# Banks dealt anew after attention, weight totals on GpSimd, small copies begun by GpSimd

## The chip, the cores and the metric

The kernel runs on one core of a Trainium2 chip. The metric is the device time of one execution in microseconds. Engines: TensorE (PE; its weight loads are PEld), VectorE (DVE), ScalarE (ACT), GpSimd (POOL), and SyncE (SP), which only begins transfers here. Each runs its instructions in the order in which they stand in its queue.

## The reference

Three stages follow one another, on 4 batches of 576 tokens with 512 features:

```python
scores = where(block_i >= block_j, q @ k.T / 8, -1e9)      # 8 heads of 64, blocks of 64
x  = softmax(scores) @ v                                   # heads side by side: (4, 576, 512)
x  = x + relu(layernorm(x) * g_ln @ w1a) @ w2a             # first FFN, 512 -> 2048 -> 512
u  = x + real(fft(fft(x, axis=1), axis=2))                 # Fourier mixing
out = u + relu(layernorm(u) @ w1b) @ w2b                   # second FFN
```

q, k, v are float32; the four weight matrices are float64, and nothing is converted on the host.

## The kernel before, in words

**Tiles.** The 2304 tokens are nine chunks of 256: for each batch b, E(b) holds tokens 0 to 255 and F(b) tokens 320 to 575 in mirrored order; L holds the 64 tokens between them of all four batches. An operand of TensorE is split into a high and a low float16 part, and a product is three passes (high-high, high-low, low-high).

**FFN.** For each chunk GEMM 1 (`gemm1`, line 482) runs in eight units mp of 24 matmuls. ScalarE writes the high half of the hidden tile hT (L491), VectorE the low half (L492). GEMM 2 (`gemm2`, L507; `gemm2_both`, L537, both 128-token halves at once, for E0 and F3 of the first FFN and E0 of the second) runs 48 matmuls a half, and VectorE adds the result to the tokens (L522). The first FFN's order is E0 E1 E2 E3 F0 F1 L F2 F3.

**Weights.** Each matrix comes in four chunks c of four pieces of 512 KB. A piece is loaded by SP (L161), decoded to float32 by two ScalarE passes (L173, L186) and two VectorE passes (L190, L193) and squared by ScalarE (L203), which gives partial sums "wn". When a chunk is whole, `w_scale` forms its total "wt" and a power-of-two scale "wsc" (`pow2`, L585 to L597); `w_hi` (L270) and `w_lo` (L279) write the two halves "wq". The total is taken by GpSimd's all-reduce (`all_sum`, L135) for the second FFN, and for the first FFN by a matmul with a tile of ones (L224), whose result lies in a PSUM buffer of tag "o". Staged chunks "ws" and scaled chunks "wq" share nine buffers of tag "w". The first FFN's eight chunks fill eight of them. Of the second FFN, two chunks of the first matrix go to DRAM and back once scaled, and those of the second matrix go there unscaled.

**Attention.** First the E chunks (`e_items`: scores L683, exponentials L701, probabilities P turned by a DMA transpose to PT, then pv, L631), while the first FFN's weights are decoded. Then, in a new SBUF pool, the other tokens (`attention_items`, scores L843, pv L631), beside which the first FFN runs chunk by chunk. `e_v` scales a batch's v by an all-reduced total "et".

**Fourier stage.** For each batch, `dft_a1` folds E and F, takes a total "dt" by all_sum, and splits the folded tokens to "ge", "gL" and "g0s"; five small SBUF copies (L1060, L1090) collect rows of gL and g0s in the tile gS. `dft_a2` multiplies ge and gS by cosine and sine matrices (ya, L1110), ScalarE and VectorE evacuate y (L1114, L1115), and `dft_b_main` does the second axis (pq, pf; L1131, L1141).

**PSUM.** Eight banks: pool psg, tag "g", two buffers of one bank (GEMM 1 and GEMM 2); pss, tag "s", two buffers of two banks (scores; later ya, pq, pf); pso, tag "o", two of one bank (pv, wt of the first FFN). all_sum's results are tiles of tag "ar" in the pool sm, which has two buffers.

**What sets the order.** The kernel's streams (E attention, weights, FFN, main attention, Fourier stage, second weights) are lists of items (planned time, function, needs, gives); `merge` calls the item with the smallest planned time next. The order of these calls is the order of the program text, and so of the priorities. The tile framework's planner then sets each engine's queue by a model of times; a buffer of a tag is given to the tiles in the order of the text. E attention of batch 0 starts at planned time 0, of batch 1 at 25, of 2 and 3 at 50; the first FFN's weights at 20, 1.6 a piece; the second matrix follows the first. The second FFN's weights start at 300, 4 a piece, and need the last attention result X1 L.

Of the kernel before, what the change touches and what calls it, by code (L numbers as in the profile page):

```python
# [8 lines left out]
F32 = mybir.dt.float32  # L9
F16 = mybir.dt.float16  # L10
# [7 lines left out]
DM = H * D  # L18
# [40 lines left out]
GB = 2  # L59
WT = ((2, 1), (2, 2))  # L60
S_E1 = 25.0
# [22 lines left out]
def fused_kernel(ctx: ExitStack, tc: tile.TileContext, io: dict):  # L84
# [8 lines left out]
    dram = ctx.enter_context(tc.tile_pool(name="dram", bufs=1, space=bass.MemoryType.DRAM))  # L93
    pss = ctx.enter_context(tc.tile_pool(name="pss", bufs=2, space=PS))
    pso = ctx.enter_context(tc.tile_pool(name="pso", bufs=4 - GB, space=PS))

    gcol = cpool.tile([128, KT], F32, name="gcol")
    gmax = cpool.tile([128, 1], F32, name="gmax")

    ones = cpool.tile([128, 128], BF16, name="ones")  # L100
    late = cpool.tile([128, 3, 128], BF16, name="late")
# [76 lines left out]
    def w_decode(ffn, which, c, i, n):  # L178
# [28 lines left out]
        )  # L207

    def w_scale(ffn, which, c):

        n2 = W.pop(("n2", ffn, which, c))
        n = n2.shape[-1]
        if (ffn, which) in WT:
            if n > 1:
                n1 = sm.tile([128, 1], F32, tag="wn1", bufs=2, name="wn1")
                nc.vector.tensor_reduce(out=n1, in_=n2, axis=AX.X, op=ALU.add)
                n2 = n1
            tot = all_sum(n2, 1, "wt")
        else:
            nb = sm.tile([128, n], BF16, tag="wnb", bufs=2, name="wnb")  # L220
            nc.vector.tensor_copy(out=nb, in_=n2)
            tot = pso.tile([128, 1], F32, tag="o", name="wt")
            for i in range(n):
                nc.tensor.matmul(  # L224
                    out=tot, lhsT=ones, rhs=nb[:, i:i + 1], start=(i == 0), stop=(i == n - 1)
                )
# [23 lines left out]
    def w_jobs(ffn, which, c):  # L250
# [5 lines left out]
        return [(st[:, i:i + m, :].rearrange("p i f -> p (i f)"), i, i + m, s) for i in range(0, 4, m)]  # L256

    def w_hi(ffn, which, c):
        if ffn == 2 and which == 1:
            t = wst["pool"].tile([128, 2, 2048], F16, tag="w", bufs=2, name=f"wq{ffn}{which}{c}")  # L260
        else:
            t = wpool.tile([128, 2, 2048], F16, tag="w", bufs=9, name=f"wq{ffn}{which}{c}")
# [10 lines left out]
        W["t", ffn, which, c] = t  # L273

# [16 lines left out]
    def w_second():  # L291


        out = []

        def piece(which, c, i):
            n = WN[1]
            w_load(2, which, c, i, n)
            w_raw(2, which, c, i, n)
            w_decode(2, which, c, i, n)  # L300
            if i + n < 4:
                return
            w_scale(2, which, c)
            if which == 1:
                w_hi(2, 1, c)
                w_lo(2, 1, c)
                if c >= 2:
                    t = W.pop((2, 1, c))
                    w_spill(t.rearrange("p a f -> p (a f)"), (2, 1, c), F16)
            else:  # L310
                st = W.pop(("st", 2, 2, c))
                w_spill(st.rearrange("p i f -> p (i f)"), (2, 2, c), F32)

        for which, order in ((1, (2, 3, 0, 1)), (2, (0, 1, 2, 3))):
            for c in order:
                for i in range(0, 4, WN[1]):
                    last = i + WN[1] == 4
                    gives = ("W", 2, 1, c) if which == 1 and last and c < 2 else None
                    if (which, c) == (2, 3) and last:
                        gives = ("W2", "dram")  # L320
# [4 lines left out]
        return out  # L325

# [16 lines left out]
    def w_items():  # L343

        n = WN[0]
        pieces = [(which, c, i) for which in (1, 2) for c in range(4) for i in range(0, 4, n)]

        def load(k):
            if k < len(pieces):
                w_load(1, *pieces[k], n)  # L350

        def piece(k):
# [4 lines left out]
            if i + n == 4:  # L357
                w_scale(1, which, c)
                if which == 1:
                    w_hi(1, which, c)  # L360
                    w_lo(1, which, c)

        def end(c):
            if c == 0:
                w_balance(1)
            w_hi(1, 2, c)
            w_lo(1, 2, c)

        first = [(0.0, lambda k=k: load(k), (), None) for k in range(PL)]
        out = ([], [])  # L370
        for k, (which, c, i) in enumerate(pieces):
            gives = ("W", 1, 1, c) if which == 1 and i + n == 4 else None
            out[which - 1].append((float(n), lambda k=k: piece(k), (), gives))
        for c in range(4):
            out[1].append((1.0, lambda c=c: end(c), (), ("W", 1, 2, c)))
        return first, out[0], out[1]
# [83 lines left out]

    def gemm1(ffn, c, mp, side=False):
        if mp == 0:
# [8 lines left out]
        xt = xnT[ffn, c]  # L471
        if side:
            ps = pss.tile([128, 2, 512], F32, tag="s", name="g1s")[:, 0, :]
            ps = ps.rearrange("p (i n) -> p i n", i=2)
        else:
            ps = psg.tile([128, 2, 256], F32, tag="g", name="g1")
        for i in range(2):
# [21 lines left out]
    def gemm2(ffn, c, t, part, nparts=4):  # L499
        if part == 0:  # L500
            g2[0] = psg.tile([128, DM], F32, tag="g", name="g2")
        ps = g2[0]
# [26 lines left out]
    def gemm2_both(ffn, c, part):  # L529

        if part == 0:
            g2["b"] = [psg.tile([128, DM], F32, tag="g", name="g2") for _ in range(2)]
        h = hT[ffn, c]
# [40 lines left out]
    def a_close():  # L574
        ap_["ctx"].close()
# [476 lines left out]
    def dft_left_split(b, s):  # L1052
# [43 lines left out]
    def dft_a2(b, blk):  # L1096
# [73 lines left out]
    def dft_b_main(b, t):  # L1170
# [3 lines left out]
        ks = slice(128 * t, 128 * t + 128)  # L1174
        pq = pss.tile([128, 512], F32, tag="s", name="pq")
        dft_b(lambda f, a: y[:, f, a, ks], lambda a: y5[:, 289 * a + 128 * t:289 * a + 128 * t + 128],
              lambda f, a: y[0:128 - f, 2 + f, a, ks], pq)
        pf = None
        if t == 0:

            pf = pss.tile([128, 512], F32, tag="s", name="pf")
            w = lambda f, a: slice(289 * (2 * f + a) + 288, 289 * (2 * f + a) + 416)
            dft_b(lambda f, a: yw[:, w(f, a)], lambda a: y5[:, w(0, a)], None, pf)
        dft_apply(pq, pf, inv[:, 0:1], X["E", b][:, t, :], X["F", b][:, t, :])

    def dft_b_left():
        yl, yl5 = D_["yl"], D_["yl5"]
        pq = pss.tile([128, 512], F32, tag="s", name="pql")
        dft_b(lambda f, a: yl[:, f, a, :], lambda a: yl5[:, a, :],
# [12 lines left out]
    if True:  # L1202
# [4 lines left out]
        nc.gpsimd.partition_all_reduce(gmax, g2c[:, KT:], 128, bass_isa.ReduceOp.max)  # L1207
        nc.vector.memset(ones, 1.0)
        nc.vector.memset(late, 0.0)
# [19 lines left out]
        def a_end():  # L1229
            a_close()  # L1230
            dft_setup(dctx)

# [10 lines left out]
        def ffn_items(ffn, order, both=(), mixed=None):  # L1243
            seq = []
            for n, c in enumerate(order):
# [3 lines left out]
                if ffn == 1 and n < LNA:  # L1249
# [6 lines left out]
                g1 = [  # L1256
                    (2.62, lambda mp=mp, c=c: gemm1(ffn, c, mp, c == mixed), (("W", ffn, 1, mp // 2),) + g1_needs,
                     ("G1", ffn, c, mp)) for mp in range(8)
# [170 lines left out]
```

## Time and profile before

| | us |
|---|---|
| median of 3 runs | 1056.16 (1055.52 to 1056.41) |
| profiled execution, its own time | 1056.17 |
| its span, first to last instruction | 1054.3 |
| TensorE busy | 943.6 (89%) |
| VectorE busy | 624.7 (59%) |
| ScalarE busy | 506.5 (48%) |
| GpSimd busy | 70.1 (7%) |

The page divides the span into 40 slices; the digit of an engine is the tenth of a slice in which it was busy, and 9 is 90% or more. A timeline row gives start, duration, engine, line, operation, tiles (out<-in), count, and in brackets the idle time before it with what ended that. A releaser is the last event by the profile; where it had long been done, the true one was another.

### The profile page before, as it was taken

To read this page: it belongs to the slowest core of one execution; us is meant where nothing else is said; L and a number is where in the kernel's file an instruction comes from. 1 tells how busy PE (TensorE), PEld (TensorE's weight loads), DVE (VectorE), ACT (ScalarE), POOL (GpSimd) and SP (SyncE) were. 2 spreads that over 40 slices of the span, in tenths; PEclk is the share of its full clock that TensorE was granted. 3 is DMA by queue.
4 is the path that set the end of the run, shared out by engine and by line. 5 is a ranking of instruction groups with operands and counts; after the bars stand their busy time and mean duration, and the time that the engine had idled before them with its cause. 6 is when DMAs were issued, how large, how long until landed. Compare 5 with 4: busy or idle time off the path is not lost.

```text
span 1054.3 us, 18458 instructions
## 1 busy us (share of the span) xinstructions
PE 943.6 (89%) x7234; PEld 644.3 (61%) x7234; DVE 624.7 (59%) x1542; ACT 506.5 (48%) x916; POOL 70.1 (7%) x190
## 2 busy tenths in 40 slices
PE   5375859998989898996999879999999999999998
PEld 4354744476566574764665655848577576585674
DVE  5778888777778876765368969864332322222210
ACT  6677876767677677525356665622111021111110
POOL 2000001001102002040000010000000000000000
PEclk9686988999999999998999999999999999999999
DMA  7887745566858657465205266520100110101100
GB/s 197 191 212 200 213 118 127 123 111 132 147 123 158 127 135 153 84 121 181 63 10 162 97 200 232 195 80 1 41 21 21 31 30 21 30 21 31 30 11 21
DMA packets 172647, 110.84 MB, mean 105 GB/s; under 512 B 146909, under 2 KB 155494, under 8 KB 171024
## 3 DMA queue, kind: packets, MB, share of 16 engines
q1 hardware_dynamic: 170880, 105.81, 40.7%
q0 software_dynamic: 1680, 3.85, 1.7%
q8 instruction: 57, 0.93, 0.4%
q14 instruction: 30, 0.25, 0.1%
HBM read 59.95 MB, written 11.01 MB: 67 GB/s over the span
## 4 chain that ended last, share of the span: by engine, by line
PE 42%; DVE 8%; DMA 5%; ACT 4%; issue 1%; POOL 0%; SPq 0%; ACTq 0%; POOLq 0%; DVEq 0%
PE g L507 19%; PE g L482 18%; DMA wr<-in_w 5%; PE g L537 2%; DVE wq L279 1%; ACT wr L203 1%; DVE ws L193 1%; ACT sign L186 1%; DVE hT L492 1%; ACT ws L173 1%; DVE ws L190 1%; PE st L843 1%; PE pv L631 1%; PE ya L1110 1%; ACT wq L270 0%
## 5 line engine op out<-in xcount | busy, mean ns | idle before, releaser
L482 PEld LDWEIGHTS <-wq 128*128 128x128 f16 x3456 | 339.6, 99 | 77.6 <-issue 27.0
L507 PE MATMUL g<-wq,hT 128*128 128x512 f16 x1440 | 331.3, 379 | 1.4 <-DVE hT L492 1.4
L507 PEld LDWEIGHTS <-hT 128*128 128x128 f16 x1440 | 139.7, 98 | 158.8 <-DVE hT L492 1.7
L491 ACT ACTIVATE hT<-g 128x512 f16<-128x512 f32 x144 | 84.7, 590 | 253.7 <-PE g L482 253.6
L492 DVE SCALAR_TENSOR_TENSOR hT<-g,hT 128x512 f16<-128x512 f32 x144 | 98.9, 688 | 145.8 <-ACT hT L491 145.8
L631 PE MATMUL pv<-vh,PT 128*128 128x65 f16 (+1 forms) x800 | 106.7, 204 | 26.3 <-DMA PT<-P 22.8
L631 PEld LDWEIGHTS <-PT 128*128 128x128 f16 x1200 | 84.3, 101 | 59.0 <-DMA PT<-P 32.5
L843 PE MATMUL st<-k,qz 128*128 128x512 f16 (+2 forms) x288 | 80.2, 338 | 11.6 <-ACT e L865 11.6
L656 DVE SCALAR_TENSOR_TENSOR P<-e,P 128x768 f16<-128x768 f32 (+2 forms) x64 | 62.0, 972 | 33.9 <-ACT P L655 33.5
L865 ACT ACTIVATE e<-st,aq,acf 128x384 f32<-128x384 f32 (+2 forms) x80 | 57.2, 742 | 50.1 <-DVE aq L860 46.3
L537 PE MATMUL g<-wq,hT 128*128 128x512 f16 x288 | 65.6, 387 | 5.2 <-ACT wq L270 3.3
L631 PE MATMUL pv<-vl,PT 128*128 128x64 f16 (+1 forms) x400 | 66.5, 203 | 0.0
L186 ACT ACTIVATE sign<-wr 128x512 f16<-128x512 f32 x64 | 49.1, 774 | 19.2 <-DMA wr<-in_w 14.0
L655 ACT ACTIVATE P<-e 128x768 f16<-128x768 f32 (+2 forms) x64 | 54.6, 858 | 3.4 <-DMA PT<-P 1.7
L173 ACT ACTIVATE ws<-wr 128x512 f32<-128x512 f32 x64 | 41.3, 667 | 31.0 <-DMA wr<-in_w 28.4
L683 PE MATMUL st<-raw 128*128 128x128 f32 (+1 forms) x128 | 39.2, 446 | 17.9 <-ACT e L701 7.5
L439 ACT ACTIVATE xs<-xn 128x512 f16<-128x512 f32 x36 | 22.5, 628 | 65.3 <-DVE xn L431 6.6
L445 DVE TENSOR_TENSOR xs<-xn,xs 128x512 f16<-128x512 f32 x36 | 24.7, 690 | 48.1 <-ACT xs L439 48.0
L537 PEld LDWEIGHTS <-hT 128*128 128x128 f16 x288 | 28.5, 99 | 39.0 <-issue 7.7
L190 DVE SCALAR_TENSOR_TENSOR ws<-ws,sign 128x512 int32<-128x512 int32 x64 | 43.3, 685 | 14.8 <-ACT sign L186 13.5
L859 DVE TENSOR_REDUCE aq<-st 128x2 f32<-128x768 f32 (+2 forms) x48 | 46.7, 973 | 0.8 <-PE st L843 0.8
L203 ACT ACTIVATE wr<-ws 128x512 bf16<-128x512 f32 (+1 forms) x40 | 35.2, 879 | 23.2 <-DVE ws L193 20.3
(387 smaller groups left out, 1291.2 us busy)
## 6 DMA issues: line engine op xcount, KB each, us to landing
wr<-in_w SPq DMA_DIRECT2D x64, 512.0 KB, 4.5
rawv<-in_vt SPq DMA_DIRECT2D x16, 320.0 KB, 3.8
rawqk<-in_kt SPq DMA_DIRECT2D x16, 288.0 KB, 2.8
out<-out SPq DMA_DIRECT2D x18, 256.0 KB, 2.0
d<-ws SPq DMA_DIRECT2D x4, 1024.0 KB, 5.5
ws<-d SPq DMA_DIRECT2D x4, 1024.0 KB, 6.8
rawqk<-in_qt SPq DMA_DIRECT2D x32, 80.0 KB, 3.7
raw<-in_qt SPq DMA_DIRECT2D x16, 128.0 KB, 3.8
```

What stands on the lines that cost most here:

```text
L186: nc.scalar.activation(out=z[:, :, :, 1], in_=hw.bitcast(F32), func=AF.Copy, scale=float(2.0 ** -100))
L190: nc.vector.scalar_tensor_tensor(out=di, in0=di, scalar=3, in1=zi, op0=ALU.logical_shift_left, op1=ALU.bitwise_or)
L482: nc.tensor.matmul(out=ps[:, i, :], lhsT=w1(ffn, k, wh, m), rhs=xt[:, xh, k, :], start=(n == 0), stop=(n == 3 * KT - 1),)
L491: nc.scalar.activation(out=h[:, :, 0, :], in_=ps, func=AF.Relu)
L492: nc.vector.scalar_tensor_tensor(out=h[:, :, 1, :], in0=ps, scalar=0.0, in1=h[:, :, 0, :], op0=ALU.max, op1=ALU.subtract,)
L507: nc.tensor.matmul(out=ps, lhsT=h[f // 4][:, f % 4, hh, t * 128:(t + 1) * 128], rhs=w2(ffn, f, wh), start=(f == 0 and hh == 0 and wh == 0) ...
L537: nc.tensor.matmul(out=g2["b"][t], lhsT=h[f // 4][:, f % 4, hh, t * 128:(t + 1) * 128], rhs=w2(ffn, f, wh), start=(f == 0 and hh == 0 and ...
L631: nc.tensor.matmul(out=out[..., 0:w], lhsT=l, rhs=v[..., 0:w], start=(n == 0), stop=(n == len(mm) - 1))
L655: nc.scalar.activation(out=P[:, 0, 0:n], in_=e, func=AF.Copy, scale=PSC)
L656: nc.vector.scalar_tensor_tensor(out=P[:, 1, 0:n], in0=e, scalar=PSC, in1=P[:, 0, 0:n], op0=ALU.mult, op1=ALU.subtract)
L843: nc.tensor.matmul(out=st[:, h, 0:n] if j < 4 else sf[:, o:o + n], lhsT=qz[:, a, q:q + 128], rhs=k[:, c, o:o + n], start=(i == 0), stop=(j ...
L865: nc.scalar.activation(out=e[:, h], in_=st[:, h], func=AF.Exp, scale=cf, bias=nb[:, h:h + 1],)
```

## The change

After attention (`ps_switch`, called from `a_end`) the pools pss and pso are closed; their six banks become psx (GX = 3 banks, for GEMM tiles) and psd (8 - 2 - 3 = 3 single banks, for the Fourier stage). GEMM tiles then go round 2 banks of psg and 3 of psx.

`w_scale` is cut in two. `w_total` takes the total by GpSimd for all weights, at the chunk's last piece. The scale and `w_hi`, `w_lo` follow one piece later, in `scales` (first FFN) and `end` (second FFN); the plan gives a chunk to its users one piece later. The tile of ones and the matmuls of L224 are gone.

The five copies to gS of a batch are begun by GpSimd, not SP. The argument `side` of gemm1 was not in use.

```diff
-WT = ((2, 1), (2, 2))
+GX = 3
-    pss = ctx.enter_context(tc.tile_pool(name="pss", bufs=2, space=PS))
-    pso = ctx.enter_context(tc.tile_pool(name="pso", bufs=4 - GB, space=PS))
+    pctx = ctx.enter_context(ExitStack())
+    pss = pctx.enter_context(tc.tile_pool(name="pss", bufs=2, space=PS))
+    pso = pctx.enter_context(tc.tile_pool(name="pso", bufs=4 - GB, space=PS))
+    psn = {"n": 0}
+    def g_tile(shape, name):
+        pool = psg
+        if "x" in psn:
+            pool = psn["x"] if psn["n"] % (GB + GX) >= GB else psg
+            psn["n"] += 1
+        return pool.tile(shape, F32, tag="g", name=name)
+    def d_tile(name):
+        return psn["d"].tile([128, 512], F32, tag="s", name=name)
+    def ps_switch():
+        pctx.close()
+        psn["d"] = pctx.enter_context(tc.tile_pool(name="psd", bufs=8 - GB - GX, space=PS))
+        psn["x"] = pctx.enter_context(tc.tile_pool(name="psx", bufs=GX, space=PS))
...
+    def w_total(ffn, which, c):
+        n2 = W.pop(("n2", ffn, which, c))
+        if n2.shape[-1] > 1:
+            n1 = sm.tile([128, 1], F32, tag="wn1", bufs=2, name="wn1")
+            nc.vector.tensor_reduce(out=n1, in_=n2, axis=AX.X, op=ALU.add)
+            n2 = n1
+        W["tot", ffn, which, c] = all_sum(n2, 1, "wt")
+        if which == 1:
+            W["t", ffn, which, c] = w_tile(ffn, which, c)
     def w_scale(ffn, which, c):
...
+        tot = W.pop(("tot", ffn, which, c))
...
         def piece(which, c, i):
             w_load(2, which, c, i, n)
             w_raw(2, which, c, i, n)
             w_decode(2, which, c, i, n)
+            end()
             if i + n < 4:
                 return
-            w_scale(2, which, c)
+            w_total(2, which, c)
...
+            todo.append((which, c))
+        def end():
+            for which, c in todo:
+                w_scale(2, which, c)
+                if which == 1:
+                    w_hi(2, 1, c)
+                    w_lo(2, 1, c)
...
         def piece(k):
             w_decode(1, which, c, i, n)
+            scales()
             if i + n == 4:
+                w_total(1, which, c)
+                todo.append((which, c))
...
-        ps = psg.tile([128, 2, 256], F32, tag="g", name="g1")
+        ps = g_tile([128, 2, 256], "g1")
...
-            nc.sync.dma_start(out=st[32 * i:32 * i + 32], in_=g[q, a])
+            nc.gpsimd.dma_start(out=st[32 * i:32 * i + 32], in_=g[q, a])
...
-            nc.sync.dma_start(out=st[96 + a:97 + a, 0:257], in_=g0s[:, a])
+            nc.gpsimd.dma_start(out=st[96 + a:97 + a, 0:257], in_=g0s[:, a])
...
-        ps = pss.tile([128, 512], F32, tag="s", name="ya")
+        ps = d_tile("ya")
...
         def a_end():
             a_close()
+            ps_switch()
             dft_setup(dctx)
```

## Rows read from the trace of the kernel before

**Rows 1.** The page's slices, TensorE's busy tenths (26.4 us a slice).
```profile
PE   5375859998989898996999879999999999999998
```
**Rows 2.** Windows: stretch, its length, each engine's busy time, granted clock, DMA.
```profile
0.00:159.00 159.00, 98.65 (x837) 80.06 (x838) 123.27 (x342) 119.17 (x211) 14.57 (x47) 0.83 0.75 188
184.00:460.00 276.00, 256.11 (x2414) 174.06 (x2412) 206.58 (x517) 189.69 (x342) 28.96 (x76) 0.99 0.65 127
481.00:515.20 34.20, 24.34 (x194) 20.14 (x192) 17.12 (x30) 19.43 (x37) 0.40 (x1) 0.85 0.42 137
515.20:552.00 36.80, 36.07 (x232) 22.33 (x231) 19.59 (x45) 15.87 (x28) 0.75 (x2) 1.00 0.08 18
552.00:688.00 136.00, 120.98 (x862) 85.30 (x862) 115.72 (x293) 87.58 (x173) 11.38 (x32) 0.99 0.53 176
```
**Rows 3.** Timeline of TensorE, GEMM 1 of L.
```profile
481.10 2.78 PE L482 MATMUL g<-xnT1L,wq 128*128 128x256 f16 x24
493.23 16.14 PE L482 MATMUL g<-xnT1L,wq 128*128 128x256 f16 x120 [9.35 <-DVE XxF L522]
...
515.22 20.88 PE L507 MATMUL g<-wq,hT 128*128 128x512 f16 x96
```
**Rows 4.** Timeline of VectorE in the same stretch.
```profile
478.18 0.75 DVE L522 SCALAR_TENSOR_TENSOR XxF<-g,winv,XxF 128x512 f32<-128x512 f32 x1
...
492.43 0.75 DVE L522 SCALAR_TENSOR_TENSOR XxF<-g,winv,XxF 128x512 f32<-128x512 f32 x1
...
496.78 0.69 DVE L492 SCALAR_TENSOR_TENSOR hT<-g,hT 128x512 f16<-128x512 f32 x1 [0.73 <-ACT hT L491]
...
506.77 0.16 DVE L216 TENSOR_REDUCE wn<-wn 128x1 f32<-128x4 f32 x1 [0.25 <-ACT wr L203]
```
**Rows 5.** Timeline of GpSimd, the all-reduces from 480 to 545 us.
```profile
487.83 0.40 POOL L135 PARTITION_ALL_REDUCE wt<-wn  x1 [17.38 <-DVE wn L216]
542.82 0.40 POOL L135 PARTITION_ALL_REDUCE dt<-dn  x1 [54.59 <-DVE dn L1072]
543.11 0.46 POOL L135 PARTITION_ALL_REDUCE wt<-wn  x1
```
**Rows 6.** Timeline of ScalarE, the first piece after chunk 3.
```profile
552.41 1.22 ACT L173 ACTIVATE ws<-wr 128x512 f32<-128x512 f32 x2 [1.39 <-DVE wq L279]
```
**Rows 7.** Timeline of TensorE, two starts between 552 and 688.
```profile
631.65 1.32 PE L1131 MATMUL pq<-c_cd,y 128*128 128x257 f16 x6 [3.81 <-DVE pw L594]
...
687.82 20.89 PE L537 MATMUL g<-wq,hT 128*128 128x512 f16 x96 [1.34 <-DVE hT L492]
```
**Rows 8.** Timeline of TensorE, totals of weight chunks five, seven and eight.
```profile
118.50 0.16 PE L224 MATMUL wt<-wnb,ones 128*128 128x1 bf16 x1
...
142.84 0.17 PE L224 MATMUL wt<-wnb,ones 128*128 128x1 bf16 x1
...
153.70 0.16 PE L224 MATMUL wt<-wnb,ones 128*128 128x1 bf16 x1 [3.44 <-DVE wnb L221]
154.51 0.23 PE L631 MATMUL pv<-vh,PT 128*128 128x65 f16 x1 [0.65 <-DMA PT<-P]
```
**Rows 9.** Timeline of SP, the main attention's first load.
```profile
168.58 0.33 SPq L767 DMA_DIRECT2D rawqk<-in_kt  x1
```
**Rows 10.** Timeline of GpSimd, et of batches 2 and 3.
```profile
65.07 0.39 POOL L135 PARTITION_ALL_REDUCE et<-en  x1 [1.28 <-ACT vh L640]
...
91.92 0.53 POOL L135 PARTITION_ALL_REDUCE et<-en  x1 [5.26 <-ACT vh L640]
```
**Rows 11.** SP's waits; groups by line; DMA issues with KB and us to landing.
```profile
SPq L1060 <- ACT g0s L1026: 33.4, 3, 25.4
...
L937 POOL DMA_DIRECT2D XxF<-N x24 | 14.0, 587 | 41.8 <-DVE N L910 31.4 <-DVE aq L860 8.2 <-ACT N L916 1.6
...
XxF<-N POOLq DMA_DIRECT2D x8, 126.0 KB, 3.8
gS<-gL SPq DMA_DIRECT2D x12, 32.0 KB, 2.0
```

More of the change, by code (lines that the diff above doesn't have):

```diff
@@ L207, in w_decode @@
         )
-    def w_scale(ffn, which, c):
[L211 to L226, printed above, removed]
+    def w_total(ffn, which, c):
[7 more added lines that the diff above has]
+            W["t", ffn, which, c] = w_tile(ffn, which, c)
+    def w_scale(ffn, which, c):
+        tot = W.pop(("tot", ffn, which, c))
         if (ffn, which) == (1, 1):
@@ L256, in w_jobs, with w_tile @@
         return [(st[:, i:i + m, :].rearrange("p i f -> p (i f)"), i, i + m, s) for i in range(0, 4, m)]
+    def w_tile(ffn, which, c):
+        if ffn == 2 and which == 1:
+            return wst["pool"].tile([128, 2, 2048], F16, tag="w", bufs=2, name=f"wq{ffn}{which}{c}")
+        return wpool.tile([128, 2, 2048], F16, tag="w", bufs=9, name=f"wq{ffn}{which}{c}")
     def w_hi(ffn, which, c):
[L259 to L262, printed above, removed]
+        if which == 2:
+            W["t", ffn, which, c] = w_tile(ffn, which, c)
+        t = W["t", ffn, which, c]
         if ffn == 1 and which == 1:
@@ L272, in w_hi @@
             )
-        W["t", ffn, which, c] = t
     def w_lo(ffn, which, c):
@@ L294, in w_second @@
         out = []
+        todo = []
         def piece(which, c, i):
@@ L300, in piece @@
             w_decode(2, which, c, i, n)
+            end()
             if i + n < 4:
                 return
-            w_scale(2, which, c)
[L304 to L310, printed above, removed]
+            w_total(2, which, c)
+            if which == 2:
                 st = W.pop(("st", 2, 2, c))
                 w_spill(st.rearrange("p i f -> p (i f)"), (2, 2, c), F32)
+            todo.append((which, c))
[5 more added lines that the diff above has]
+                    w_lo(2, 1, c)
+                    if c >= 2:
+                        t = W.pop((2, 1, c))
+                        w_spill(t.rearrange("p a f -> p (a f)"), (2, 1, c), F16)
+            todo.clear()
         for which, order in ((1, (2, 3, 0, 1)), (2, (0, 1, 2, 3))):
@@ L316, in w_second @@
                 for i in range(0, 4, WN[1]):
[L317 to L320, printed above, removed]
+                    gives = None
+                    if i == 0 and (which, c) in ((1, 1), (2, 0)):
+                        gives = ("W", 2, 1, 0 if which == 1 else 1)
                     needs = (("X1", "L"),)
@@ L324, in w_second @@
                     ))
-        return out
+        return out + [(0.0, end, (), ("W2", "dram"))]
     def w_back(c):
@@ L350, in load @@
                 w_load(1, *pieces[k], n)
+        todo = []
         def piece(k):
@@ L356, in piece, with scales @@
             w_decode(1, which, c, i, n)
+            scales()
             if i + n == 4:
+                w_total(1, which, c)
+                todo.append((which, c))
+        def scales():
+            for which, c in todo:
                 w_scale(1, which, c)
@@ L361, in piece @@
                     w_lo(1, which, c)
+            todo.clear()
         def end(c):
             if c == 0:
+                scales()
                 w_balance(1)
@@ L371, in w_items @@
         for k, (which, c, i) in enumerate(pieces):
-            gives = ("W", 1, 1, c) if which == 1 and i + n == 4 else None
+            gives = ("W", 1, 1, c - 1) if which == 1 and i == 0 and c > 0 else None
             out[which - 1].append((float(n), lambda k=k: piece(k), (), gives))
+        out[0].append((0.0, scales, (), ("W", 1, 1, 3)))
         for c in range(4):
@@ L459, in run, with gemm1 @@
             f()
-    def gemm1(ffn, c, mp, side=False):
+    def gemm1(ffn, c, mp):
         if mp == 0:
@@ L471, in gemm1 @@
         xt = xnT[ffn, c]
[L472 to L475, printed above, removed]
-            ps = psg.tile([128, 2, 256], F32, tag="g", name="g1")
+        ps = g_tile([128, 2, 256], "g1")
         for i in range(2):
@@ L500, in gemm2 @@
         if part == 0:
-            g2[0] = psg.tile([128, DM], F32, tag="g", name="g2")
+            g2[0] = g_tile([128, DM], "g2")
         ps = g2[0]
@@ L531, in gemm2_both @@
         if part == 0:
-            g2["b"] = [psg.tile([128, DM], F32, tag="g", name="g2") for _ in range(2)]
+            g2["b"] = [g_tile([128, DM], "g2") for _ in range(2)]
         h = hT[ffn, c]
@@ L1174, in dft_b_main @@
         ks = slice(128 * t, 128 * t + 128)
-        pq = pss.tile([128, 512], F32, tag="s", name="pq")
+        pq = d_tile("pq")
         dft_b(lambda f, a: y[:, f, a, ks], lambda a: y5[:, 289 * a + 128 * t:289 * a + 128 * t + 128],
@@ L1179, in dft_b_main @@
         if t == 0:
-            pf = pss.tile([128, 512], F32, tag="s", name="pf")
+            pf = d_tile("pf")
             w = lambda f, a: slice(289 * (2 * f + a) + 288, 289 * (2 * f + a) + 416)
@@ L1187, in dft_b_left @@
         yl, yl5 = D_["yl"], D_["yl5"]
-        pq = pss.tile([128, 512], F32, tag="s", name="pql")
+        pq = d_tile("pql")
         dft_b(lambda f, a: yl[:, f, a, :], lambda a: yl5[:, a, :],
@@ L1207, in fused_kernel @@
         nc.gpsimd.partition_all_reduce(gmax, g2c[:, KT:], 128, bass_isa.ReduceOp.max)
-        nc.vector.memset(ones, 1.0)
         nc.vector.memset(late, 0.0)
@@ L1256, in ffn_items @@
                 g1 = [
-                    (2.62, lambda mp=mp, c=c: gemm1(ffn, c, mp, c == mixed), (("W", ffn, 1, mp // 2),) + g1_needs,
+                    (2.62, lambda mp=mp, c=c: gemm1(ffn, c, mp), (("W", ffn, 1, mp // 2),) + g1_needs,
                      ("G1", ffn, c, mp)) for mp in range(8)
```

1 line of the change is left out of this document (removed).

## The prediction

> **What bounds the kernel now.** I read the slices of the page first, then the busy time by stage, then the waits stage by stage. The slices show the reader a TensorE that is full from slice 27 to the end and ragged before it [rows 1]: whatever the change gains must be gained before about 690 us, by feeding TensorE sooner. The stages say how much there is [rows 2]: TensorE is idle for 60.3 us of the first 159 us (weights of the first FFN, attention of the first 256 tokens), for 19.9 us of the main attention (184 to 460), for 9.9 us between 481 and 515.2, 0.7 us to 552, and 15.0 us between 552 and 688. Idle time is a gain only where no other chain sets the end of the stage, so each stage is taken by itself.
>
> 481 to 515: TensorE computes GEMM 1 of chunk L. Its first unit goes through at 481.10, then it waits 9.35 us for XxF, the evacuation of the GEMM 2 before it, because "g" has two banks [rows 3]. That evacuation stands on VectorE behind the scale and low parts of a weight chunk and comes at 492.43 [rows 4]. What follows the wait is slow as well: the granted clock of the stage is 0.85 [rows 2], and the 120 matmuls after the gap take 16.14 us where 24 before it took 2.78 us [rows 3] (13.9 us by that pace): after 9 us of idleness part of them ran at the lower level (1.2 GHz, not 2.4).
>
> 515 to 688: the weights of the second FFN. Chunk 3's partial sums are ready at 506.77 [rows 4], but GpSimd takes its total at 543.11, after the Fourier total dt that waited 54.59 us [rows 5]. Both are tiles of the tag "ar" with two buffers, and buffers of a tag are dealt in the order in which the program text asks for them: by the merge, dft_a1(0) comes between chunks 2 and 3. So 36 us pass, and only when chunk 3 has been scaled does its staging buffer come free: the next piece starts at 552.41, released by VectorE's wq [rows 6]. (Eight of the nine "w" buffers hold the first FFN.) From there VectorE is busy 115.7 of 136 us [rows 2], and the chain ends in TensorE's GEMM 2 of E0 at 687.82, released by VectorE's last hT [rows 7], after which nothing stops TensorE. dt hangs on chunk L's GEMM 2, so what L gains, this chain gains.
>
> 0 to 184: the eight totals on TensorE share the tag "o" with the pv tiles, and run in exactly the merged order: the last total at 153.70 (TensorE idle 3.44 us before it) and pv of (3,1) right behind it at 154.51, though it needs nothing of it [rows 8]. The main attention's first load goes out at 168.58 [rows 9], when the last pv is through.
>
> **The change part by part.** *Banks.* After attention GEMM tiles go round five banks (2 old, 3 new). With F1's two GEMM 2 halves in the first two (the first is evacuated at 478.18), units 0 to 3 of L run without a wait: 481.10 + 4 x 2.7 = 491.9. Unit 4 needs the bank freed at 492.43 + 0.75 = 493.2, ends at 495.9; unit 5 needs unit 0's evacuation, at 496.78 + 0.69 = 497.5 in today's order; 6 and 7 follow: 505.6 against 515.22 [rows 3, 4]. That is 9.6 us, with only two gaps of 1.3 and 1.6 us left, so the slow clock goes too. Bounds: 0, if the planner lets hT of L stand still later on VectorE, and 481.10 + 8 x 2.7 = 502.7, 12.5 us. I take 9.6, as it keeps today's VectorE order. dt, chunk 3's total, wq and the restart at 552.41 move by the same 9.6 us [rows 5, 6].
> The Fourier stage gets three single banks for two double ones. The row nearest to it is the wait of 3.81 us at 631.65 [rows 7]; it ends on small VectorE work, which banks don't shorten. Of the 15.0 us idle after 552, short hT waits go, but VectorE at 85% remains: between 0 and 15, I take 1.5.
>
> *Sums on GpSimd, scale a piece later.* Eight totals leave TensorE: the matmuls are 0.16 us each, and TensorE's waits for them (3.44 us before the last) lie in a stage where it has 60 us to spare. What counts is who stood behind: pv. New is that the eight totals share "ar" with the four et totals of the first attention. By the merge's clock the totals stand at 24.8, 31.2, 37.6, 44, 50.4, 56.8, 63.2, 69.6 and et at 3, 28, 53, 67. So et of batch 2 (now 65.07) comes after the fifth total (now 118.50), and et of batch 3 (now 91.92) after the seventh (142.84) [rows 8, 10]; behind each et stand the scales of v. pv of (2,0) then comes some 4 us (an estimate from hT's 0.69 us for 512 columns [rows 4]: two passes over 1024 and small steps) later than the 118.5 at which "o" now holds it, the first pv of batch 3 at about 147, but (3,1) to (3,3) no longer wait for the eighth total. I put the end near 158 to 162 instead of 168, and the gain in the main attention's 19.9 us of idle time at 3 us: it cannot exceed 10, and where et's turn comes late it is a loss (rival 3). Scaling a piece later delays a chunk of the first FFN's first matrix by one piece, 146/32 = 4.6 us from the 32 loads in the stage; the cover is TensorE's spare time, since GEMM 2 of E0 waits for the second matrix, whose last scale is not put off. In the second FFN, first matrix, the later scale cannot take effect: with one staging buffer the next piece still waits for the low part [rows 6]. In its second matrix VectorE no longer waits for the total before going on; those waits are under a microsecond, counted 0.
>
> *Copies begun by GpSimd.* Twenty small copies leave SP, which today stands up to 25.4 us on them (33.4 us in three waits) [rows 11]. In that long wait, 520 to 546, the two load buffers were full and the staging buffer taken until 552, so it cost nothing; the later ones are a few microseconds. GpSimd needs 0.59 us for each such start, 5 x 0.59 = 2.9 us per batch, and lands them later: 3.8 us against 2.0 us [rows 11], though with larger transfers. TensorE's ya needs them, so a batch may lose up to 1.8 us, three batches 5.4 (the fourth lies under GEMM 2 of E0); the other end is a gain of some 5 us where SP's loads were behind. GpSimd's queue has behind them qc, yl and the next totals; it is nearly empty. I take +1.5 us.
> The Trainium skill speaks against this step ("SBUF — State Buffer", Who interferes with whom): a VectorE instruction in a two-port mode shuts GpSimd out for its whole length, so a software-started DMA can be starved. The 24 starts of the main attention, beside a VectorE busy 206.6 of 276 us, show no such thing at a mean of 0.59 us [rows 2, 11]; by the rule alone each of 15 starts could wait out an instruction as long as hT (0.69 us [rows 4]), an estimate of 10 us, and the sum would be -2 us.
>
> *Sum.* -9.6 - 1.5 - 3 + 1.5 = -12.6 us. The profiled execution took 1056.17 us (span 1054.3 and 1.9 around it), as good as the median 1056.16. 1056.2 - 12.6 = 1043.6 us.
>
> **The rivals.** *1. The second FFN's weights come off the path.* If the first attention ends 10 us earlier and that passes through the main one, the weights start earlier against TensorE's work; then most of the 9.9 + 0.7 + 15.0 us and the slow clock's 2.2 go, with 3: 1056 - 29 = 1027 to 1032. For it: VectorE has 17.2 us free between 515 and 552 [rows 2]. Against: dt still bars chunk 3.
> *2. The gain is taken back.* Banks only let TensorE run ahead; if the planner's new order puts dt, or the copies, before more of the weights on GpSimd, GEMM 2 of E0 still starts at about 685: 1053 to 1056. For it: the end of that stage hangs on VectorE, not on TensorE [rows 7].
> *3. Slower: et's turn.* The v scales of batches 2 and 3 now wait for the fifth and seventh total. If each such turn also holds a GpSimd memset or an SP load behind it (the one turn that the trace shows, dt before chunk 3, cost 36 us [rows 5]), pv of batch 3 ends 20 us after today's instead of 8 before. The main attention starts 20 us later; TensorE has a GEMM 2 of 20.9 us [rows 7] to cover part of it; I let 15 pass: -9.6 + 15 + 1.5 = +7, 1063 us. It decides when the last pv comes later than about 178.
> *4. The banks don't do it.* If L's units keep stopping on hT instead, the term is 3 instead of 9.6: about 1050.
>
> **How the numbers follow.** Forecast (1036 to 1047) 0.48; rival 1 (1024 to 1036) 0.16; rival 4 (1047 to 1053.5) 0.13; rival 2 0.10, most of it within 0.2%; rival 3 0.13. Faster by over 0.2% (about what this kernel's runs can tell from no change): 0.48 + 0.16 + 0.13 + 0.01 = 0.78; within 0.2%: 0.08; slower: 0.14. The range reaches from rival 1's middle to the edge of rival 2: 1028 to 1056, leaving out some 0.05 below and 0.15 above.
>
> **What would show it.** Right: no wait over 3 us of GEMM 1 on XxF after 481; GEMM 2 of L about 10 us earlier, dt and chunk 3's total still side by side and earlier by the same; GEMM 2 of E0 starting near 676 to 680; the last pv of batch 3 before 165; the first ya of a batch waiting 1 to 2 us for gS. Wrong: chunk 3's total no longer behind dt (then rival 1), a first load of the main attention after 170 (rival 3), or TensorE idle again after GEMM 2 of E0.

## The result and the profile after

The changed kernel takes 1045.02 us (median of 5, 1043.08 to 1050.94) beside 1055.55 us of the kernel before in the same runs: ratio 0.9895, 95% interval 0.9873 to 0.9916. The forecast was 1043.6 us. The profiled execution took 1044.0 us with a span of 1042.2; lines of the profile after are those of the changed kernel (GEMM 1 L515, GEMM 2 L540 and L570, all-reduces L153).

The windows of the kernel after, with the columns of [rows 2]:
```profile
0.00:159.00 159.00, 107.43 (x858) 82.99 (x859) 127.50 (x341) 124.44 (x216) 17.70 (x55) 0.84 0.77 192
184.00:460.00 276.00, 256.85 (x2401) 174.76 (x2399) 207.21 (x530) 187.27 (x338) 31.71 (x79) 0.98 0.65 129
481.00:515.20 34.20, 30.23 (x212) 20.45 (x210) 18.00 (x33) 17.65 (x34) 0.40 (x1) 1.00 0.47 138
515.20:552.00 36.80, 36.80 (x276) 26.84 (x275) 25.72 (x56) 20.52 (x38) 3.36 (x7) 1.00 0.25 68
552.00:688.00 136.00, 120.93 (x803) 81.81 (x801) 114.46 (x290) 84.47 (x166) 16.87 (x47) 0.94 0.53 167
```
The stretch of chunk L has lost 5.9 of its 9.9 us of idle time, and its low clock (1.00, not 0.85). The stretch from 552 to 688 is as idle as before, 15.1 of 136 us, and its granted clock is now lower: 0.94, not 0.99. With the banks alone it is 0.95. That this costs time is not shown: the kernel with four new banks, below, has 0.99 there, and its way from GEMM 2 of L to GEMM 2 of E0 is no shorter (169.5 us beside 168.0).

The timeline of TensorE, GEMM 1 of L to its GEMM 2, answers to [rows 3]; the last row is GEMM 2 of E0 in the second FFN and answers to [rows 7]:
```profile
475.72 10.64 PE L515 MATMUL g<-xnT1L,wq 128*128 128x256 f16 x96
488.12 2.78 PE L515 MATMUL g<-xnT1L,wq 128*128 128x256 f16 x24 [1.75 <-DVE XxF L555]
492.11 5.40 PE L515 MATMUL g<-xnT1L,wq 128*128 128x256 f16 x48 [1.22 <-DVE hT L525]
498.51 2.78 PE L515 MATMUL g<-xnT1L,wq 128*128 128x256 f16 x24 [1.00 <-DVE hT L525]
501.13 20.88 PE L540 MATMUL g<-wq,hT 128*128 128x512 f16 x96
...
674.21 15.70 PE L570 MATMUL g<-wq,hT 128*128 128x512 f16 x72
```
Four units go through without a stop, and the wait for XxF falls from 9.35 to 1.75 us. GEMM 1 of L takes 25.4 us where it took 34.1.

The timeline of GpSimd, all-reduces, answers to [rows 5, 8, 10]:
```profile
106.33 0.38 POOL L153 PARTITION_ALL_REDUCE wt<-wn  x1 [14.33 <-ACT wr L221]
106.61 0.46 POOL L153 PARTITION_ALL_REDUCE et<-en  x1
...
143.51 0.38 POOL L153 PARTITION_ALL_REDUCE wt<-wn  x1 [11.95 <-ACT wr L221]
...
482.20 0.40 POOL L153 PARTITION_ALL_REDUCE wt<-wn  x1 [16.83 <-DVE wn L232]
528.74 0.39 POOL L153 PARTITION_ALL_REDUCE dt<-dn  x1 [46.13 <-DVE dn L1105]
529.03 0.46 POOL L153 PARTITION_ALL_REDUCE wt<-wn  x1
```
The eighth total of the first FFN's weights comes at 143.5, 10.2 us earlier. dt and chunk 3's total still stand side by side, 14.1 us earlier. The first load of the main attention on SP answers to [rows 9]:
```profile
160.99 0.34 SPq L800 DMA_DIRECT2D rawqk<-in_kt  x1
```

With these starts the span is cut into stretches. F1, L and E0 are chunks; E0's GEMM 2 is that of the second FFN. Each row of the table is one profiled execution, in us; the experiments are told below.

| kernel | first load | to GEMM 2 of F1 | to GEMM 2 of L | to GEMM 2 of E0 | to the end |
|---|---|---|---|---|---|
| before | 168.6 | 291.8 | 54.8 | 172.6 | 366.5 |
| after | 161.0 | 294.0 | 46.1 | 173.1 | 368.0 |
| after, second trial | 157.8 | 294.8 | 46.2 | 171.2 | 368.0 |
| banks alone | 167.5 | 291.6 | 47.1 | 169.7 | 368.3 |
| totals by GpSimd alone | 162.0 | 293.7 | 54.7 | 171.7 | 366.8 |
| banks, totals by GpSimd | 164.2 | 297.4 | 45.9 | 168.9 | 368.5 |
| and later scale, first FFN alone | 159.2 | 294.7 | 47.4 | 168.2 | 368.0 |
| the same, totals by TensorE | 156.3 | 292.5 | 46.3 | 168.0 | 368.0 |

Before to after: -7.6 + 2.2 - 8.7 + 0.5 + 1.5 = -12.1 us, the difference of the spans. The 1.5 at the end is work that changed sides: in the kernel before, fourteen matmuls of ya of batch 3 ran ahead of GEMM 2 of E0, now behind its start. The last two columns are therefore read together: 539.1 before, 541.1 after.

### The profile page after: what moved, and what is told of

Its sections match the earlier page's. It is cut to its first block, busy times and chain, and to the rows that moved or that the text cites. A ratio compares the mean times of both kernels' runs of the same rounds, so it can differ in the third digit from the quotient of the medians.

```text
span 1042.2 us, 18427 instructions
## 1 busy us (share of the span) xinstructions
PE 948.7 (91%) x7226; PEld 647.6 (62%) x7226; DVE 622.7 (60%) x1533; ACT 505.0 (48%) x916; POOL 82.0 (8%) x218
## 4 chain that ended last, share of the span: by engine, by line
PE 43%; DVE 7%; DMA 6%; ACT 4%; issue 1%; POOL 0%; SPq 0%; ACTq 0%
PE g L540 19%; PE g L515 19%; DMA wr<-in_w 6%; PE g L570 2%; ACT wr L221 1%; DVE ws L211 1%; DVE ws L208 1%; DVE hT L525 1%; ACT sign L204 1%; PE ya L1143 1%; PE pv L664 1%; PE st L876 1%; ACT ws L191 1%; PE pq L1174 0%; PE pq L1164 0%
## 5 line engine op out<-in xcount | busy, mean ns | idle before, releaser
L515 PEld LDWEIGHTS <-wq 128*128 128x128 f16 x3456 | 339.0, 99 | 73.5 <-issue 15.9
L540 PE MATMUL g<-wq,hT 128*128 128x512 f16 x1440 | 332.1, 380 | 1.4 <-DVE hT L525 1.4
L540 PEld LDWEIGHTS <-hT 128*128 128x128 f16 x1440 | 140.0, 98 | 160.3 <-DVE hT L525 1.6
L570 PE MATMUL g<-wq,hT 128*128 128x512 f16 x288 | 65.7, 388 | 2.3 <-DVE ln1('E', 2)_2196 L439 2.3
L482 DVE TENSOR_TENSOR xs<-xn,xs 128x512 f16<-128x512 f32 x36 | 24.7, 688 | 46.4 <-ACT xs L476 46.3
L570 PEld LDWEIGHTS <-hT 128*128 128x128 f16 x288 | 28.6, 100 | 36.2 <-DVE ln1('E', 2)_2196 L439 2.4
```

The source lines that it names most:

```text
L515: nc.tensor.matmul(out=ps[:, i, :], lhsT=w1(ffn, k, wh, m), rhs=xt[:, xh, k, :], start=(n == 0), stop=(n == 3 * KT - 1),)
L540: nc.tensor.matmul(out=ps, lhsT=h[f // 4][:, f % 4, hh, t * 128:(t + 1) * 128], rhs=w2(ffn, f, wh), start=(f == 0 and hh == 0 and wh == 0) ...
L570: nc.tensor.matmul(out=g2["b"][t], lhsT=h[f // 4][:, f % 4, hh, t * 128:(t + 1) * 128], rhs=w2(ffn, f, wh), start=(f == 0 and hh == 0 and ...
```

## The experiments

Each ratio is to the kernel before, run on the same chip in the same rounds. The first four experiments ran beside each other, and so did the next four and the last four, each group on a chip of its own; across groups only the ratios are compared.

**Banks alone.** The kernel before, with `g_tile`, `d_tile` and `ps_switch` of the change:
```diff
-        ps = pss.tile([128, 512], F32, tag="s", name="ya")
+        ps = d_tile("ya")
...
             a_close()
+            ps_switch()
```


> The kernel before with the banks dealt anew after attention, and nothing else. Theory (the banks are one of two independent gains): GEMM 1 of chunk L loses its 9.35 us wait and takes about 25.5 us instead of 34, dt and the total of chunk 3 come side by side 8 to 9 us earlier (near 534), GEMM 2 of E0 starts near 679; the last pv of batch 3 stays near 168. Time -8.5 us, 1047. Rival (the banks pay only because the weights of the first FFN come earlier): the wait goes, but the time lies in a later wait of the second FFN's weights; -3 us or less, 1053 or more. Rival (the Fourier stage loses by three single banks for two double ones): as the first, but idle time of TensorE between 552 and 688 rises by 3 us or more, -5 us, 1051.

Measured: ratio 0.9902 (0.9879 to 0.9925). The timeline of TensorE in chunk L, and GEMM 2 of E0:
```profile
479.83 10.64 PE L498 MATMUL g<-xnT1L,wq 128*128 128x256 f16 x96
492.96 2.78 PE L498 MATMUL g<-xnT1L,wq 128*128 128x256 f16 x24 [2.48 <-DVE XxF L538]
...
506.17 20.88 PE L523 MATMUL g<-wq,hT 128*128 128x512 f16 x96
...
675.82 15.70 PE L553 MATMUL g<-wq,hT 128*128 128x512 f16 x72
```
GEMM 1 of L takes 26.3 us, the first load stays at 167.5. The banks are a gain of their own of about 10 us: most of what the whole change gives (1.05% above, 1.35% in a second trial below). Neither rival holds.

**Totals by GpSimd alone.**
```diff
-WT = ((2, 1), (2, 2))
+WT = ((1, 1), (1, 2), (2, 1), (2, 2))
```


> The kernel before with the eight totals of the first FFN's weights taken by GpSimd; the scale stays where it was, no bank and no copy is touched. Theory (what held the first stage was the turn in the tag o, which tied the totals to pv): the totals come about 10 us earlier (the last near 144 instead of 153.7), the first load of the main attention near 161 instead of 168.6, of which some 5 us are left at the start of chunk L: -5 us, 1051. Rival (the scale a piece later is what took the time away): VectorE now stands in wait for each total before it goes on, the first load of the main attention comes at 165 or later and the time is within 2 us of before. Rival (as the prediction had it, 3 us for the whole): -3 us, 1053.

Measured: ratio 0.9969 (0.9949 to 0.9988), 3.3 us by it. The first load comes at 162.03, the last total at 149.09. By size it is the third answer, what the prediction said of the whole; the theory's 5 us lie just inside the interval's edge.

**Copies by SP again.**
```diff
-            nc.gpsimd.dma_start(out=st[32 * i:32 * i + 32], in_=g[q, a])
+            nc.sync.dma_start(out=st[32 * i:32 * i + 32], in_=g[q, a])
```
(and the copies of g0s likewise.)

> The changed kernel with the twenty small copies to gS begun by SP again. Theory from the trace of the changed kernel (TensorE's ya shows no wait for gS there, and after 552 TensorE's idle time did not change): the copies are worth nothing either way, within 2 us of the changed kernel, 1043 to 1047. The prediction's term (copies by GpSimd cost 1.5 us): 1.5 us faster, 1043.5. Rival (SP's loads of the second FFN stood behind the copies, and that cost as soon as chunk 3 comes earlier): 3 to 5 us slower than the changed kernel, 1048 to 1050.

Measured: ratio 0.9867 (0.9841 to 0.9893), against 0.9895 (0.9873 to 0.9916) and, in a second trial below, 0.9865 (0.9835 to 0.9895) with the copies on GpSimd. No difference can be told; the rival's 3 to 5 us slower did not come.

**Own result buffers for wt, et and dt.**
```diff
-        r = sm.tile([128, n], F32, tag="ar", name=name)
+        r = sm.tile([128, n], F32, tag="ar" + name, name=name)
```


> The changed kernel with two result buffers each for the totals wt, et and dt instead of two for all three. Theory (buffers of one tag go round in the order of the text, and dt bars the total of chunk 3): chunk 3's total comes before 505 instead of at 529.0, the weights of the second FFN run some 20 us ahead, TensorE's 15 us of idle time between 552 and 688 falls to 5 to 8, GEMM 2 of E0 starts near 666: 8 us faster than the changed kernel, 1037. In the first attention et of batches 2 and 3 no longer stand behind the fifth and seventh total: up to 3 us more. Rival (VectorE and the loads are the limit, dt was only in front of them): the total comes early, but the pieces after it, bound by VectorE, take the place, and the time stays within 2 us of the changed kernel.

Measured: ratio 0.996 (0.9942 to 0.9978), some 7 us slower than the changed kernel's 0.9895 (0.9873 to 0.9916). The all-reduces of GpSimd, one window, and TensorE's unit of F2's GEMM 1 that waits longest, then GEMM 2 of E0:
```profile
502.85 0.39 POOL L153 PARTITION_ALL_REDUCE wt<-wn  x1 [19.04 <-DVE wn L232]
521.40 0.38 POOL L153 PARTITION_ALL_REDUCE wt<-wn  x1 [18.16 <-DVE wn L232]
544.80 0.76 POOL L153 PARTITION_ALL_REDUCE dt<-dn  x1 [23.01 <-DVE dn L1105]
```
```profile
515.20:552.00 36.80, 30.79 (x235) 22.72 (x234) 26.69 (x61) 28.06 (x53) 4.49 (x9) 1.00 0.41 111
```
```profile
538.52 2.78 PE L515 MATMUL g<-xnT1('F', 2)_6535,wq 128*128 128x256 f16 x24 [2.61 <-DVE XxL L555]
...
683.07 15.70 PE L570 MATMUL g<-wq,hT 128*128 128x512 f16 x72
```
The turn is real: with it gone, chunk 3's total comes 26 us earlier, at 502.85. But nothing is gained, and my theory fell here. The pieces that no longer wait are decoded by VectorE and ScalarE beside L and F2 (ScalarE 28.1 us of that window, 20.5 in the changed kernel), TensorE is now idle for 6.0 us there, and the first dt, which all of the Fourier stage hangs on, comes 16 us later. The idle time after 552 stays at 14.7 us, for it is not the weights: its waits are those of the Fourier stage for its own evacuations y. By this reading, which no further run tested, the turn held the weights back where they would have been in the way. In the first attention et of batches 2 and 3 now comes at 58.27 and 103.32, not 106.61 and 131.10, and the first load at 161.36, in the changed kernel at 160.99: no cost of et's late turn can be seen.

**The changed kernel again.**

> The changed kernel once more, beside the next three on the same chip, as their standard of comparison: 0.9895 of the kernel before, 0.987 to 0.992. Its stretch from GEMM 2 of L to GEMM 2 of E0 in the second FFN: 172.9 us again if that length belongs to the kernel; near 169.6, as with the banks alone, if it only differed by chance.

Measured: ratio 0.9865 (0.9835 to 0.9895); stretch 171.2 us, nearer to 172.9 than to 169.6.

**No later scale.** Banks as above, all totals by GpSimd, copies by SP; the diffs are those of the first two experiments together.

> The kernel before with two of the three parts in their plainest form: banks dealt anew and all totals by GpSimd, the scale at once, the copies by SP. Theory (banks and totals are independent and add up, -0.98% and -0.31%; the later scale and the copies by GpSimd bring nothing or cost a little): ratio 0.987, 1043, which is the changed kernel or 2 to 3 us better. Rival (the later scale is a part of the gain, VectorE stands in wait for the totals without it): the totals add nothing to the banks, ratio 0.990 to 0.992, slower than the changed kernel.

Measured: ratio 0.9906 (0.9881 to 0.993), no better than the banks alone. The rival holds: taken together with the banks, totals by GpSimd add nothing that can be seen.

**Later scale in the first FFN alone.** The changed kernel, with the second FFN's scale back in its piece:
```diff
             w_total(2, which, c)
...
+            w_scale(2, which, c)
+            if which == 1:
+                w_hi(2, 1, c)
+                w_lo(2, 1, c)
...
-            todo.append((which, c))
```
(and the plan gives the chunk to its users a piece earlier again.)

> The changed kernel with the scale of the second FFN's weights at once again, that of the first FFN still a piece later. Theory (the stretch from GEMM 2 of L to GEMM 2 of E0 takes 172.9 us in the changed kernel and 169.6 with the banks alone, and the later scale is what differs in it, next to the copies, which took 172.4 when they were SP's): the stretch falls to about 170 and the time by 2 to 3 us, 1042. Rival (the prediction's term: the later scale cannot take effect in the second FFN): within 1 us of the changed kernel.

Measured: ratio 0.984 (0.9817 to 0.9862), beside 0.9865 (0.9835 to 0.9895) of the changed kernel on the same chip; the intervals overlap. The stretch, from the timelines of TensorE, first the changed kernel in its second trial, then this one:
```profile
498.74 20.88 PE L540 MATMUL g<-wq,hT 128*128 128x512 f16 x96
...
669.96 15.70 PE L570 MATMUL g<-wq,hT 128*128 128x512 f16 x72
```
```profile
501.34 20.88 PE L533 MATMUL g<-wq,hT 128*128 128x512 f16 x96
...
669.50 15.70 PE L563 MATMUL g<-wq,hT 128*128 128x512 f16 x72
```
171.2 us against 168.2. With the end taken in, the four profiles that have new banks and the later scale in both FFNs (the changed kernel twice, with copies by SP, with two new banks; own result buffers left aside) stand at 538.1 to 541.1 us, the seven that have new banks without it in the second at 536.0 to 537.9: means of 539.8 and 536.8. So the later scale of the second FFN costs some 3 us. In this pair it is idle time of TensorE (14.7 us of the stretch against 11.7, at a granted clock of 0.96 in both), and it is seen in TensorE's waits from 552 to 688 (us in total, times, longest), of the changed kernel's second trial and of this one:
```profile
PE ya L1143 <- DVE y L1148: 3.9, 1, 3.9
```
```profile
PE ya L1136 <- DVE y L1141: 0.5, 1, 0.5
```
Why these y come late is not shown: in the changed kernel's second trial batch 2's y stand on VectorE from 651.53 to 656.13, and the last step of a scale (wsc) at 636.34 and 658.21, with no low part between.

**Two new banks.** The changed kernel with `GX = 2`.

> The changed kernel with two new banks for the GEMMs instead of three, so four in all, and four for the Fourier stage instead of three. Theory (in chunk L each bank is worth one unit of 2.7 us of headstart, and the Fourier stage does not want banks but its evacuations): unit 3 of L now waits for XxF, the wait there grows from 1.75 to about 4.4 us, TensorE's idle time between 552 and 688 stays near 15: 2.5 us slower than the changed kernel, 1047. Rival (the Fourier stage lacks banks: its ya waited 4.5 us for evacuations and pq 7.8): 3 to 5 us come back there, and the kernel is faster than the changed one by 1 to 2 us.

Measured: ratio 0.9917 (0.9897 to 0.9937), 5 us slower than the changed kernel beside it. TensorE in chunk L:
```profile
472.86 8.02 PE L515 MATMUL g<-xnT1L,wq 128*128 128x256 f16 x72
486.49 15.93 PE L515 MATMUL g<-xnT1L,wq 128*128 128x256 f16 x120 [5.60 <-DVE XxF L555]
```
Three units of headstart instead of four, as expected, and a wait of 5.60 us. The loss is larger than the one unit because the 120 matmuls behind the wait take 15.93 us; the kernel with four new banks below has 120 in 13.26.

**The best so far again.**

> The version that was fastest so far (later scale in the first FFN alone), once more as the standard of the next three on the same chip: ratio 0.984, 0.981 to 0.987, and a stretch from GEMM 2 of L to GEMM 2 of E0 of 168 us. If it comes out at 0.988 or more, its lead over the changed kernel was chance.

Measured: ratio 0.9855 (0.9832 to 0.9877), stretch 168.0 us.

**Four new banks.** The same version with `GX = 4`.

> That version with four new banks for the GEMMs and two for the Fourier stage. Theory (from two new banks to three, chunk L gained 4 us; a fourth can only take the last wait for XxF, and two banks make every ya and pq of the Fourier stage wait for the evacuation before it): XxF's wait of 2.8 us in chunk L goes, TensorE's idle time between 552 and 688 rises from 11.7 to 15 or more: 1 to 4 us slower than the standard. Rival (the Fourier stage waits for its evacuations, banks don't matter there): 2 us faster than the standard.

Measured: ratio 0.9859 (0.9824 to 0.9895), no difference that can be told. TensorE in chunk L:
```profile
469.81 13.26 PE L508 MATMUL g<-xnT1L,wq 128*128 128x256 f16 x120
483.31 2.78 PE L508 MATMUL g<-xnT1L,wq 128*128 128x256 f16 x24 [0.23 <-DVE XxF L548]
487.48 5.40 PE L508 MATMUL g<-xnT1L,wq 128*128 128x256 f16 x48 [1.39 <-DVE hT L518]
495.18 23.15 PE L533 MATMUL g<-wq,hT 128*128 128x512 f16 x96 [2.30 <-DVE hT L518]
```
The wait for XxF goes to 0.23 us, but the waits for hT (1.39 and 2.30 us) take its place and chunk L takes 46.1 us as with three. In the Fourier stage TensorE's idle time from 552 to 688 is 11.6 us, not the 15 or more that the theory asked for. By the times its 1 to 4 us are not seen, though 4 us lie within the uncertainty.

**Copies by SP, without the later scale of the second FFN.**

> That version with the twenty copies to gS begun by SP. Theory (the copies are worth nothing either way, as in the first trial): within 1.5 us of the standard, ratio 0.983 to 0.986. The prediction's term: 1.5 us faster. Rival (SP's queue holds loads of the second FFN behind the copies): 2 us slower or more.

Measured: ratio 0.984 (0.9823 to 0.9857), stretch 168.1 us: again no difference that can be told from GpSimd (0.9855, 0.9832 to 0.9877, beside it). This kernel differs from "no later scale" by the later scale of the first FFN alone (with the plan's later handing over that belongs to it): 0.984 against 0.9906 (0.9881 to 0.993), 0.66%, about 7 us. The version with GpSimd's copies, on the chip of "no later scale", has 0.984 as well.

**Totals by TensorE, later scale.** The version with the later scale in the first FFN, its totals back in the tag "o":
```diff
-        W["tot", ffn, which, c] = all_sum(n2, 1, "wt")
+        nb = sm.tile([128, n], BF16, tag="wnb", bufs=2, name="wnb")
+        nc.vector.tensor_copy(out=nb, in_=n2)
+        tot = pso.tile([128, 1], F32, tag="o", name="wt")
+        for i in range(n):
+            nc.tensor.matmul(
+                out=tot, lhsT=ones, rhs=nb[:, i:i + 1], start=(i == 0), stop=(i == n - 1)
+            )
+        W["tot", ffn, which, c] = tot
```


> That version with the totals of the first FFN taken by TensorE again, in the tag o, the scale still a piece later. Theory (the gain of the first stage comes from taking the totals out of the tag o and TensorE's queue, where each stands between two pv; the scale a piece later holds the buffer of the total even longer): the first load of the main attention comes at 166 us or later, as in the kernel before, and the ratio is 0.990 or worse, that of the banks alone. Rival (the later scale is the gain, whoever takes the total): first load near 160, ratio 0.984 to 0.986.

Measured: ratio 0.9814 (0.9794 to 0.9834), median 1035.63 us: the fastest of all, below the changed kernel's 0.9835 to 0.9895; the version with GpSimd's totals beside it has 0.9855 (0.9832 to 0.9877). The rival holds, and my reading of the first stage falls. SP's first load, then VectorE's wait for the squares of a chunk (20 to 165 us; us in total, times, longest), in the kernel before and in this one:
```profile
156.27 0.34 SPq L805 DMA_DIRECT2D rawqk<-in_kt  x1
```
```profile
DVE wnb L221 <- ACT wr L203: 6.6, 3, 4.1
```
```profile
DVE wnb L240 <- ACT wr L222: 1.0, 3, 0.4
```
The totals are TensorE's and share the tag with pv as in the kernel before, yet the last of them comes at 141.9, not 153.7. What is gone is VectorE standing for ScalarE's squares with the next piece behind it. With the totals on GpSimd and the scale at once (totals by GpSimd alone, same window) the wait sat elsewhere, in ScalarE before the high half:
```profile
ACT wq L270 <- DVE gs L265: 5.0, 3, 3.0
```
It is 1.6 us in the changed kernel. That these waits make the whole gain is not shown; that the later scale makes it is.

## Why the prediction was right, step by step

The time was right, its closeness in part by luck. The profile's 12.1 us are 8.7 in chunk L (forecast 9.6), 5.4 ahead of it (forecast 3), and 2.0 lost behind it (forecast -1.5 + 1.5 = 0): misses of +0.9, -2.4 and +2.0 us that nearly cancel. The banks, the largest term, were right for the reason given; what lies ahead of chunk L was not.

*Banks: -9.6.* Right in mechanism and nearly in size: the stretch of L lost 8.7 us, and 7.8 with the banks alone. Unit 4 stopped for XxF and two later units for hT, as worked out. Of the signs that it named, no wait for XxF over 3 us came, and GEMM 2 of E0 started at 674.2, a little before the 676 to 680. Mis-sized were the gaps: three that sum to 3.97 us, not two of 1.3 and 1.6.

*After 552: -1.5.* The banks alone moved the two last stretches from 539.1 to 537.9, so 1.2 us by one profile each. In the changed kernel this is covered by the later scale of the second FFN. Of that step the prediction said that it "cannot take effect"; that failed: it cost some 3 us. The start of the next piece, which the prediction looked at, is not what moved: it comes 9.9 us behind chunk 3's total (538.93 behind 529.03), 9.3 us in the kernel before [rows 5, 6]. The time is lost later, in TensorE's wait for the y of the Fourier stage; what puts these y late is not shown.

*Copies: +1.5.* Neither shown nor excluded: two pairs show no difference, with some 3 us of uncertainty each. The reason given is not borne out: GpSimd's copies landed in 1.7 us (median of 12 of 32 KB), those of SP in 2.0 [rows 11], where the prediction had taken 3.8 from larger transfers, and in the changed kernel TensorE's ya waits for y alone from 552 to 688, never for gS. The Trainium skill's rule against the step ("SBUF — State Buffer", Who interferes with whom), that VectorE can starve software-started DMAs, is not seen: beside a VectorE busy 114.5 of 136 us the starts took
```profile
L1093 POOL DMA_DIRECT2D gS<-gL x12 | 6.3, 526 | 12.0 <-ACT gL L1059 8.4 <-DVE invL L1118 3.4 <-issue 0.2
```
0.53 us each. The estimate of 10 us that hung on it is out. The trace does not say which of VectorE's instructions ran in such a mode.

*Sums on GpSimd, scale a piece later: -3.* The step that failed is the cause: "What counts is who stood behind: pv." In the profile the first load came 7.6 us earlier, of which 2.2 were lost in the main attention, so 5.4, not 3. The gain belongs to the later scale, which the prediction had at nothing: 0.66% (no later scale against later scale in the first FFN), while GpSimd's totals are worth 0.31% without the banks, nothing beside them, and with the later scale TensorE's totals do at least as well (0.9794 to 0.9834 against 0.9832 to 0.9877 and 0.9817 to 0.9862). The prediction followed one chain (total, tag "o", pv) because the trace showed the order there; but the row of that pv names the transposed PT, not the total, as what ended its wait [rows 8], and that VectorE's queue stood for a chunk's squares, 6.6 us in three waits, was in the same trace and not read.

*Rivals.* Rival 2's "gain taken back" did not come, nor rival 4. Rival 3's turn came just as described, et of batch 2 right behind the fifth total at 106.6, with no cost that can be seen. Rival 1 expected 24 to 29 us once the second FFN's weights come off the path; taking dt out of their way gave the opposite, since that stage's idle time hangs on the Fourier stage's evacuations.

*Not settled.* Whether GpSimd's totals really cost against TensorE's, and where; how much of the later scale's gain is each wait; what takes 2 to 3 us back in the main attention when it starts earlier.

## What to carry to other kernels

When a statistic over a whole chunk gates a scale, put the scale an item later in program order, so that the in-order engine has the next item's work in front of the wait; then it matters little which engine takes the statistic. This is no rule for every stage: in the second FFN the same step cost some 3 us. Give the banks of a finished stage to the one that stops on evacuations, and stop at the number where the next wait (here hT) takes over. A buffer turn that holds work back, here a total for some 27 us (its sums ready at 501.5, taken at 529.0), can be useful: before removing it, ask whose engines the released work will take.

## What the runs showed of the hardware that was not expected

The changed kernel and five variants of it (copies by SP, two new banks, the later scale in the first FFN alone, this with copies by SP and with four new banks) have the same queues on all engines until long after the first attention. Their eight profiles have the first load anywhere from 154.7 to 163.1 us. One profile of that stage can't tell a gain of 5 us; the times over rounds can.

Some waits of TensorE cost more than their length. GEMM 1 matmuls of 256 columns run 24 in 2.78 us, 72 in 8.02, 120 in 13.26. Behind the waits for XxF of 1.1 to 2.8 us in seven of the profiles (1.75 in the changed kernel) they do so too. Behind others they do not; TensorE in chunk L with totals by GpSimd alone, copies by SP, own result buffers, and copies by SP without the later scale of the second FFN:
```profile
488.36 9.89 PE L482 MATMUL g<-xnT1L,wq 128*128 128x256 f16 x72 [9.17 <-DVE XxF L522]
493.01 10.30 PE L515 MATMUL g<-xnT1L,wq 128*128 128x256 f16 x72 [4.17 <-DVE XxF L555]
489.32 9.54 PE L515 MATMUL g<-xnT1L,wq 128*128 128x256 f16 x72 [2.47 <-DVE XxF L555]
486.38 4.13 PE L508 MATMUL g<-xnT1L,wq 128*128 128x256 f16 x24 [3.74 <-DVE XxF L548]
```
Behind 5.60 and 9.35 us, 120 took 15.93 and 16.14. These six waits cost another 1.4 to 2.9 us, and their length alone does not set it: 2.47 us cost 1.5 more, 2.78 us (later scale in the first FFN alone) nothing, 9.17 us 1.9. In the kernel with four new banks GEMM 2 of L, behind waits of 0.23, 1.39 and 2.30 us, took 23.15 us, not 20.88. The stretch 481 to 515.2 has a granted clock, a mean of the levels of 1.2 and 2.4 GHz, of 0.85 to 0.95 in these seven kernels, and 1.00 (2.4 GHz throughout) in the seven others.
